# Local and global attention followed by an RWKV feed-forward: sigmoid as tanh, the softmax inverse and the squares moved to VectorE

## The chip, the core and the metric

The kernel runs on one core of a Trainium2 chip. A core has a matrix engine (PE, whose weight loads are listed apart as PEld), VectorE (DVE), ScalarE (ACT), GpSimd (POOL) and SyncE (SP, which issues the DMAs). Each engine works through its own queue strictly in order; semaphores tie the queues together. The metric is the device time of one execution in microseconds (us), lower is better.

## The reference

The attention has 8 batches, 8 heads, 512 local and 32 global positions, head dimension 64. A global query attends to everything; a local one to the 32 global keys and to local keys within 32 positions. Its output, joined over the heads, is the input of the feed-forward:

```
a = exp(s - max(s)) / (sum(exp(s - max(s))) + 1e-9)       # softmax, both kinds of query
x = attention output as (8, 576, 512)
xk = mu_k * x + (1 - mu_k) * x_prev                        # x_prev: one position earlier
xr = mu_r * x + (1 - mu_r) * x_prev
k = maximum(xk @ w_k, 0)                                   # 512 -> 1024
v = k * k @ w_v                                            # 1024 -> 512
out = 1 / (1 + exp(-(xr @ w_r))) * v
```

Everything is float32. The kernel keeps that accuracy by splitting each operand of a product into a high and a low part and adding three products.

## The kernel before

**Staging.** A unit is one batch and two heads; four units make a batch. While the heads of batch b are computed, the feed-forward of batch b-1 runs beside them; `together` interleaves the two generator streams in program order. From batch 2 on (`FROM`) the value product is done for two halves of 256 tokens at once by a Strassen scheme (class `Keys`), which needs sums and differences of the squared keys (`differences`, L624). At the end the 32 global tokens of all batches go through the feed-forward.

**What orders the work.** The kernel is written with a tile framework that schedules the whole program itself: it takes the instructions, simulates their progress on the engines with its own costs, and writes each engine's queue. So an edit in one line can move instructions everywhere. `tc.high_priority()` brings an instruction forward.

**The softmax of a unit** (`scores`). PE writes eight score blocks into four PSUM banks (L351). VectorE adds the mask, scales and takes the minimum of the negated scores (L320, eight times). ScalarE computes eight exponentials with their sums (L326). For each half `e` of the eight blocks `inverse` is called once: ScalarE adds 1e-9 to four sums (L283), VectorE takes the reciprocal (L284), and POOL multiplies the half by it (L335, a large and a small piece). PE then transposes the four blocks of each half (L372) into a bank, which ScalarE (half 0) or VectorE (half 1) copies out (L374), and two more blocks (L381) follow through the same banks. `scores_global` does the like for the global queries (L399 to L409).

**The feed-forward.** `mix` forms xk and xr on VectorE (L509, L513) and splits them (ScalarE L517, POOL L518). Products go into PSUM banks of the tag "m": two in the first stage, three from batch 2 on, seven at the very end. For the keys, ScalarE takes relu out of the bank. In batches 0 and 1 (`keys_and_gate`) POOL squares it in SBUF (L532) and ScalarE squares it again for the high part (L535). From batch 2 on (`squares`) ScalarE's relu (L551) goes to SBUF and POOL squares it there (L552). The bank is free when ScalarE has read it.

**The gate** (`gates`). For batch 0 ScalarE takes the sigmoid straight from each of the two banks (L564). For all later tokens VectorE copies each bank to SBUF (L568) and ScalarE takes one sigmoid over both (L570). ScalarE's functions come in sets, and only one set is loaded: a change between exponential and sigmoid is an instruction of its own, ACT_TABLE_LOAD, which the compiler places. `write` and `values` multiply gate and value (L582, L590) and store.

**Weights.** Each chunk of weights arrives as 64-bit words and is decoded by ScalarE (L190), VectorE (L191 to L197), ScalarE (L203) and POOL (L204); three buffers take turns, so the next load waits for POOL's last step.

Of the kernel before, what the change touches and what calls it, by code (L numbers as in the profile page):

```python
# [9 lines left out]
F32 = mybir.dt.float32  # L10
# [5 lines left out]
AF = mybir.ActivationFunctionType  # L16
# [3 lines left out]
P = 128  # L20
# [35 lines left out]
def local_global_attention_then_rwkv_ffn(  # L56
# [12 lines left out]
    nc = tc.nc  # L69
# [5 lines left out]
    scale = 1.0 / D ** 0.5  # L75

    const = ctx.enter_context(tc.tile_pool(name="const", bufs=1))
# [60 lines left out]

    mu_k_sb = const.tile([P, NC], F32, name="mu_k_sb")
    mu_r_sb = const.tile([P, NC], F32, name="mu_r_sb")  # L140
    eps = const.tile([P, 1], F32, name="eps")
    nc.vector.memset(eps, 1e-9)


    xg_all = const.tile([P, NC, GB, SG + 1], F32, name="xg_all")
# [76 lines left out]
    HC = NF // 2  # L222
# [57 lines left out]

    def inverse(ssum):

        nc.scalar.activation(ssum, ssum, AF.Identity, bias=eps)  # L283
        nc.vector.reciprocal(ssum, ssum)  # L284
        return ssum

# [10 lines left out]
    def scores(slots):  # L297

        r = Scores(slots)
        Pt = att2.tile([P, 8, WG], F32, tag="Pt", name="Pt")  # L300
        Pgl = att2.tile([P, 2, 4, SG], F32, tag="Pgl", name="Pgl")
        low_x = small.tile([P, 8], F32, tag="m", name="m")
        ssum = small.tile([P, 8], F32, tag="ssum", name="ssum")

        banks = [psum("s") for _ in range(4)]

        def place(e, t, h):
            return banks[2 * h + e][:, t * WG:(t + 1) * WG]
        run = Run(reads["s"] if slots[0][0].b > 1 else None)
        for t, (s, p) in enumerate(slots):  # L310
            for e in range(2):
                for a, i in enumerate(PAIRS[e][p]):
                    for h in range(2):
                        rows = slice(h * D, (h + 1) * D)
                        run.matmul(
                            place(e, t, h)[a * BL:(a + 1) * BL], s.q[rows, i * BL:(i + 1) * BL],
                            s.k[rows, START[i]:START[i] + WG], start=True, stop=True,
                        )
        for e, t, h, i in EACH:
            read = nc.vector.tensor_tensor_reduce(  # L320
                out=Pt[:, i], in0=place(e, t, h), in1=masks[:, e, slots[t][1]], op0=ALU.add, op1=ALU.min,
                scale=-scale, scalar=HUGE, accum_out=low_x[:, i:i + 1],
            )
        reads["s"] = [read]
        for e, t, h, i in EACH:
            nc.scalar.activation(  # L326
                Pt[:, i], Pt[:, i], AF.Exp, bias=low_x[:, i:i + 1], scale=-1.0, accum_out=ssum[:, i:i + 1],
            )
        for e in range(2):
            each = slice(4 * e, 4 * e + 4)  # L330
            rinv = inverse(ssum[:, each])
            window = Pt[:, each, SG * e:SG * e + W]
            for out, at in ((window, SG * e), (Pgl[:, e], 0 if e else W)):
                n = out.shape[2]
                nc.gpsimd.tensor_mul(out, Pt[:, each, at:at + n], rinv.unsqueeze(2).to_broadcast([P, 4, n]))  # L335
        r.Pt, r.Pgl = Pt, Pgl
        return r
# [150 lines left out]
    class Tokens:  # L488
# [29 lines left out]
                    nc.gpsimd.tensor_sub(lo[:, both], xf, hi[:, both].bitcast(F32))  # L518
            (_, self.xk_h, self.xk_l), (_, self.xr_h, self.xr_l) = got

        def keys_and_gate(self, whole_gate=True):

            self.kk_h, self.kk_l = [], []
            for f0 in range(0, NF, 2):
                kp = psum("m").rearrange("p (j n) -> p j n", j=2)
                for j in range(2):
                    products(kp[:, j], wk_h, wk_l, slice((f0 + j) * P, (f0 + j + 1) * P),
                             lambda c: self.xk_h[:, c], lambda c: self.xk_l[:, c], NC)
                rk = self.two(tmpp, "relu")
                nc.scalar.activation(rk, kp, AF.Relu)  # L530
                k2 = self.two(tmpp, "k2")
                nc.gpsimd.tensor_mul(k2, rk, rk)  # L532
                kh = self.two(mlp, "kkh", F32R, f"kkh{f0}")
# [6 lines left out]
            yield from self.gates(whole_gate)  # L540

        def squares(self, k2):

            for f0 in range(0, NF, 2):
                kp = psum("m").rearrange("p (j n) -> p j n", j=2)
                for j in range(2):
                    products(kp[:, j], wk_h, wk_l, slice((f0 + j) * P, (f0 + j + 1) * P),
                             lambda c: self.xk_h[:, c], lambda c: self.xk_l[:, c], NC)
                rk = self.two(tmpp, "relu")
                with tc.high_priority():  # L550
                    nc.scalar.activation(rk, kp, AF.Relu)  # L551
                nc.gpsimd.tensor_mul(k2[f0 // HC][f0 % HC // 2], rk, rk)  # L552
                yield

        def gates(self, whole_gate=True, pool=None):
            pool = pool or gatep
            self.gate = pool.tile([P, NC, TOK], F32, tag="gate", name="gate")
            for e0 in range(0, NC, 2):
                rp = psum("m").rearrange("p (j n) -> p j n", j=2)
                for j in range(2):  # L560
                    products(rp[:, j], wr_h, wr_l, slice((e0 + j) * P, (e0 + j + 1) * P),
                             lambda c: self.xr_h[:, c], lambda c: self.xr_l[:, c], NC)
                if not whole_gate:
                    nc.scalar.activation(self.gate[:, e0:e0 + 2], rp, AF.Sigmoid)  # L564
                    yield
                    continue
                with tc.high_priority(None if pool is not gatep else 0):
                    nc.vector.tensor_copy(self.gate[:, e0:e0 + 2], rp)  # L568
                if e0 + 2 == NC:
                    nc.scalar.activation(self.gate, self.gate, AF.Sigmoid)  # L570
                yield

        def values(self):
# [224 lines left out]
    def tokens_of(b):  # L798
        return [local_tokens(b, half, [xT_of(b, c) for c in range(NC)]) for half in range(2)]
# [21 lines left out]
    keys = [t.keys_and_gate(whole_gate=False) for t in first]  # L821
    decoding = weights(range(EARLY), wk_h, wk_l, "m")

    def by_halves(pair, p):
# [124 lines left out]
    t, = final.tokens  # L949
# [74 lines left out]
```

## Time and profile before

| | us |
|---|---|
| three timed runs | 713.49, 715.49, 715.31 (median 715.31) |
| profiled execution, its own time | 713.44 |
| its span in the profile | 711.6 |
| PE busy | 673.6 (95%) |
| VectorE, ScalarE, POOL busy | 404.2, 421.2, 412.1 |
| granted PE clock, mean over the span | 0.976 |

Busy time is the sum of an engine's instructions without overlap. A group of instructions is shown with its line, engine, operation, output and inputs, count, busy time and mean duration, and then with the idle time of that engine just before these instructions and what ended it. The stage tables give each engine's busy time in a stretch of the span, the granted clock of PE (1.00 is full) and the share of the DMA engines.

### The profile page before, as it was taken

To read this page: it belongs to the slowest core of one execution; us is meant where nothing else is said; L and a number is where in the kernel's file an instruction comes from. 1 tells how busy PE (TensorE), PEld (TensorE's weight loads), DVE (VectorE), ACT (ScalarE), POOL (GpSimd) and SP (SyncE) were. 2 spreads that over 40 slices of the span, in tenths; PEclk is the share of its full clock that TensorE was granted. 3 is DMA by queue.
4 is the path that set the end of the run, shared out by engine and by line. 5 is a ranking of instruction groups with operands and counts; after the bars stand their busy time and mean duration, and the time that the engine had idled before them with its cause. 6 is when DMAs were issued, how large, how long until landed. Compare 5 with 4: busy or idle time off the path is not lost.

```text
span 711.6 us, 18686 instructions
## 1 busy us (share of the span) xinstructions
PE 673.6 (95%) x7472; PEld 629.5 (88%) x7472; DVE 404.2 (57%) x1180; ACT 421.2 (59%) x1135; POOL 412.1 (58%) x415
## 2 busy tenths in 40 slices
PE   5779899998999999899999999999999999999997
PEld 3558788888999999889999999999989999999896
DVE  5757986535635473755665465726673557276341
ACT  5857786646656557755748384857466654442430
POOL 6556597785534356575557656575559434854820
PEclk9679999999999999999999999999999999999999
DMA  8631678554312541271918174544736090544665
GB/s 346 277 119 43 240 213 285 197 186 130 138 56 96 180 162 72 98 258 44 357 47 309 49 284 161 220 138 174 273 115 242 2 354 3 193 137 147 198 193 201
DMA packets 43543, 123.37 MB, mean 173 GB/s; under 512 B 4032, under 2 KB 20928, under 8 KB 43456
## 3 DMA queue, kind: packets, MB, share of 16 engines
q1 hardware_dynamic: 43456, 122.18, 48.7%
q8 instruction: 59, 0.97, 0.5%
q14 instruction: 28, 0.23, 0.1%
HBM read 104.86 MB, written 17.30 MB: 172 GB/s over the span
## 4 chain that ended last, share of the span: by engine, by line
PE 56%; ACT 13%; DVE 9%; POOL 8%; DMA 6%; issue 6%; SPq 0%; POOLq 0%; ACTq 0%; DVEq 0%
PE ps_m L643 13%; PE ps_m L486 9%; PE ps_m L485 9%; PE ps_m L484 9%; PE ps_s L351 8%; ACT Pt L326 4%; DVE xfull L513 3%; DMA w<-w_v 3%; PE ps_t L372 2%; POOL B L552 2%; DVE diff L509 2%; POOL Pt L335 1%; DMA w<-w_r 1%; PE ps_s L353 1%; DVE B L624 1%
## 5 line engine op out<-in xcount | busy, mean ns | idle before, releaser
L484 PE MATMUL ps_m<-xkh,wk_h 128*128 128x256 f32 x544 | 154.2, 285 | 6.7 <-ACT xkh L517 2.4
L485 PE MATMUL ps_m<-xkl,wk_h 128*128 128x256 f32 x544 | 152.0, 280 | 1.3 <-POOL xkl L518 1.3
L486 PE MATMUL ps_m<-xkh,wk_l 128*128 128x256 f32 x544 | 152.3, 280 | 0.0
L643 PE MATMUL ps_m<-bh,a 128*128 128x256 f32 x736 | 137.8, 283 | 1.5 <-DMA a<-scratch 0.8
L643 PEld LDWEIGHTS ps_m<-bh,a 128*128 128x128 f32 x736 | 115.6, 190 | 3.4 <-issue 1.6
L326 ACT ACTIVATE Pt<-Pt,m 128x160 f32<-128x160 f32 x256 | 106.5, 419 | 16.4 <-DVE m L320 13.9
L484 PEld LDWEIGHTS ps_m<-xkh,wk_h 128*128 128x128 f32 x544 | 102.7, 189 | 9.5 <-ACT xkh L517 2.9
L335 POOL TENSOR_TENSOR Pt<-Pt,ssum 128x512 f32<-128x512 f32 x64 | 70.5, 1102 | 69.3 <-DVE ssum L284 66.7
L485 PEld LDWEIGHTS ps_m<-xkl,wk_h 128*128 128x128 f32 x544 | 102.9, 189 | 1.8 <-POOL xkl L518 1.8
L643 PE MATMUL ps_m<-bl,a 128*128 128x256 f32 x368 | 103.6, 281 | 0.0
L486 PEld LDWEIGHTS ps_m<-xkh,wk_l 128*128 128x128 f32 x544 | 102.8, 189 | 0.0
L518 POOL TENSOR_TENSOR xkl<-xfull,xkh 128x512 fp32r<-128x512 f32 x34 | 45.3, 1333 | 60.7 <-ACT xkh L517 45.7
L552 POOL TENSOR_TENSOR B<-relu 128x512 f32<-128x512 f32 x52 | 56.6, 1095 | 40.2 <-ACT relu L551 40.1
L484 PE MATMUL ps_m<-xrh,wr_h 128*128 128x256 f32 x272 | 79.1, 291 | 0.0
L486 PE MATMUL ps_m<-xrh,wr_l 128*128 128x256 f32 x272 | 78.5, 290 | 0.1
L485 PE MATMUL ps_m<-xrl,wr_h 128*128 128x256 f32 x272 | 77.9, 287 | 0.0
L551 ACT ACTIVATE relu<-ps_m 128x512 f32<-128x512 f32 x52 | 31.0, 595 | 76.2 <-PE ps_m L486 76.2
L643 PEld LDWEIGHTS ps_m<-bl,a 128*128 128x128 f32 x368 | 69.8, 190 | 0.6 <-issue 0.6
L320 DVE CUSTOM_DVE_ANT_0 Pt<-ps_s,masks 128x160 f32<-128x160 f32 x256 | 65.6, 317 | 3.2 <-PE ps_s L351 3.0
L509 DVE TENSOR_TENSOR diff<-xT 128x256 f32<-128x256 f32 x64 | 38.7, 642 | 32.7 <-ACT xT L476 18.9
L203 ACT CAST bh<-B 128x512 fp32r<-128x512 f32 x76 | 45.5, 625 | 16.3 <-PE ps_m L643 13.8
L486 PEld LDWEIGHTS ps_m<-xrh,wr_l 128*128 128x128 f32 x272 | 52.5, 193 | 3.0 <-issue 2.8
(144 smaller groups left out, 1631.5 us busy)
## 6 DMA issues: line engine op xcount, KB each, us to landing
a<-scratch SPq DMA_DIRECT2D x92, 512.0 KB, 5.8
raw_qk<-qk SPq DMA_DIRECT2D x32, 768.0 KB, 5.5
raw_v<-v SPq DMA_DIRECT2D x32, 640.0 KB, 5.1
out_l<-gate SPq DMA_DIRECT2D x32, 256.0 KB, 4.7
w<-w_k SPq DMA_DIRECT2D x8, 512.0 KB, 9.9
w<-w_v SPq DMA_DIRECT2D x8, 512.0 KB, 5.5
w<-w_r SPq DMA_DIRECT2D x4, 512.0 KB, 4.6
scratch<-wv_h SPq DMA_DIRECT2D x8, 256.0 KB, 4.0
```

The source lines that it names most:

```text
L203: nc.scalar.copy(hi, val)
L320: read = nc.vector.tensor_tensor_reduce(out=Pt[:, i], in0=place(e, t, h), in1=masks[:, e, slots[t][1]], op0=ALU.add, op1=ALU.min, scale=-s ...
L326: nc.scalar.activation(Pt[:, i], Pt[:, i], AF.Exp, bias=low_x[:, i:i + 1], scale=-1.0, accum_out=ssum[:, i:i + 1],)
L335: nc.gpsimd.tensor_mul(out, Pt[:, each, at:at + n], rinv.unsqueeze(2).to_broadcast([P, 4, n]))
L351: self.last = nc.tensor.matmul(*a, **kw)
L484: nc.tensor.matmul(out, w_h[:, i, cols], x_h(i), start=(i == 0), stop=False)
L485: nc.tensor.matmul(out, w_h[:, i, cols], x_l(i), start=False, stop=False)
L486: nc.tensor.matmul(out, w_l[:, i, cols], x_h(i), start=False, stop=(i == n - 1))
L509: nc.vector.tensor_sub(self.shape(diff[:, j]), self.cur(c0 + j), self.prev(c0 + j))
L518: nc.gpsimd.tensor_sub(lo[:, both], xf, hi[:, both].bitcast(F32))
L552: nc.gpsimd.tensor_mul(k2[f0 // HC][f0 % HC // 2], rk, rk)
L643: nc.tensor.matmul(out[:, j], w, x[:, i % 2], start=fresh and (i, j, n) == (0, 0, 0), stop=(i, n) == (HC - 1, 2), skip_group_check=True,)
```

## The change

Three edits, and one consequence of the first:

- The gate is computed as 1/2 + tanh(x/2)/2. ScalarE takes the tanh with scale 0.5 straight from each PSUM bank, and then one Copy with scale 0.5 and bias 0.5 over the whole gate. This holds for all tokens; the special case of batch 0 and VectorE's copy out of the bank are gone.
- `inverse` adds 1e-9 on VectorE. In `scores` it is called once for all eight sums, after the eighth exponential, where it was called for each half.
- From batch 2 on the square of the keys is a product of the PSUM bank and relu, on VectorE with high priority, where it was a product of relu with itself on POOL. The bank is then free when VectorE has read it.

Names of the tiles and all other functions stay. Line numbers behind the edits fall by one to four.

```diff
-    eps = const.tile([P, 1], F32, name="eps")
-    nc.vector.memset(eps, 1e-9)
...
     def inverse(ssum):
-        nc.scalar.activation(ssum, ssum, AF.Identity, bias=eps)
+        nc.vector.tensor_scalar_add(ssum, ssum, 1e-9)
         nc.vector.reciprocal(ssum, ssum)
         return ssum
...
+        all_inv = inverse(ssum)
         for e in range(2):
             each = slice(4 * e, 4 * e + 4)
-            rinv = inverse(ssum[:, each])
+            rinv = all_inv[:, each]
...
                 rk = self.two(tmpp, "relu")
                 with tc.high_priority():
                     nc.scalar.activation(rk, kp, AF.Relu)
-                nc.gpsimd.tensor_mul(k2[f0 // HC][f0 % HC // 2], rk, rk)
+                with tc.high_priority():
+                    nc.vector.tensor_mul(k2[f0 // HC][f0 % HC // 2], kp, rk)
                 yield
...
-                if not whole_gate:
-                    nc.scalar.activation(self.gate[:, e0:e0 + 2], rp, AF.Sigmoid)
-                    yield
-                    continue
                 with tc.high_priority(None if pool is not gatep else 0):
-                    nc.vector.tensor_copy(self.gate[:, e0:e0 + 2], rp)
+                    nc.scalar.activation(self.gate[:, e0:e0 + 2], rp, AF.Tanh, scale=0.5)
                 if e0 + 2 == NC:
-                    nc.scalar.activation(self.gate, self.gate, AF.Sigmoid)
+                    nc.scalar.activation(self.gate, self.gate, AF.Copy, scale=0.5, bias=0.5)
                 yield
```

The order in which the engines take their instructions moves with it. The first place is ScalarE's queue at the first gate of batch 0. (`Pt`, `Pg` are softmax weights, `w` a chunk of weights, `ps_m` a PSUM bank.) Before:

```order
L190 ACTIVATE w_856<-w_856 128x512
L564 ACT_TABLE_LOAD
L564 ACTIVATE gate<-ps_m 128x512
L283 ACTIVATE ssum<-ssum,eps 128x4
L517 CAST xrh<-xfull 128x512
L564 ACTIVATE gate<-ps_m 128x512
L374 COPY PT<-ps_t 128x512
L517 CAST xkh<-xfull 128x512
L407 ACT_TABLE_LOAD
L407 ACTIVATE Pg,ssumg<-Pg,mg 128x576
```

With the change:

```order
L324 ACTIVATE Pt,ssum<-Pt,m 128x160 x4
L564 ACTIVATE gate<-ps_m 128x512
L516 CAST xkh<-xfull 128x512
L516 CAST xrh<-xfull 128x512
L564 ACTIVATE gate<-ps_m 128x512
L373 COPY PT<-ps_t 128x512
L406 ACTIVATE Pg,ssumg<-Pg,mg 128x576
L566 ACTIVATE gate<-gate 128x1024
```

Both table loads and the inverse are gone from this stretch, and one instruction, L566, has come in. In the whole program there were 30 table loads; now there is one, the first.

The second place is VectorE's queue at the differences of the squared keys of batch 2, the first batch of the Strassen scheme (`B_...` and `T_...` are blocks of squared keys and their differences, `PT` is the copy out of the transposes' bank). Before:

```order
L284 RECIPROCAL ssum<-ssum 128x4 x2
L624 TENSOR_TENSOR B_3407<-B_3842,B_3407 128x512
L624 TENSOR_TENSOR B_3407<-B_3843,B_3407 128x512
L624 TENSOR_TENSOR T_4051<-B_3844,B_3407 128x512
L624 TENSOR_TENSOR B_3842<-B_3844,B_3842 128x512
L374 COPY PT<-ps_t 128x512
```

With the change:

```order
L551 TENSOR_TENSOR B_3808<-ps_m,relu 128x512
L281 TENSOR_SCALAR ssum<-ssum 128x8
L620 TENSOR_TENSOR B_3377<-B_3808,B_3377 128x512
L282 RECIPROCAL ssum<-ssum 128x8
L551 TENSOR_TENSOR B_3809<-ps_m,relu 128x512
L620 TENSOR_TENSOR B_3377<-B_3809,B_3377 128x512
L551 TENSOR_TENSOR B_3810<-ps_m,relu 128x512
L620 TENSOR_TENSOR T_4015<-B_3810,B_3377 128x512
L620 TENSOR_TENSOR B_3808<-B_3810,B_3808 128x512
L620 TENSOR_TENSOR B_3378<-B_3378,T_4015 128x512
L373 COPY PT<-ps_t 128x512
```

The three squares now stand between the differences that need them; the two steps of the inverse stand among them too, and one more difference is ahead of the copy.

The third place is POOL's queue at the same squares. Before:

```order
L552 TENSOR_TENSOR B_3842<-relu 128x512
L335 TENSOR_TENSOR Pt<-Pt,ssum 128x4x128
L335 TENSOR_TENSOR Pgl<-Pt,ssum 128x128
L335 TENSOR_TENSOR Pt<-Pt,ssum 128x4x128
L335 TENSOR_TENSOR Pgl<-Pt,ssum 128x128
L552 TENSOR_TENSOR B_3843<-relu 128x512
L552 TENSOR_TENSOR B_3844<-relu 128x512
L552 TENSOR_TENSOR B_3845<-relu 128x512
L204 TENSOR_TENSOR bl<-T_4051,bh 128x512
```

With the change:

```order
L334 TENSOR_TENSOR Pt<-Pt,ssum 128x4x128
L334 TENSOR_TENSOR Pgl<-Pt,ssum 128x128
L334 TENSOR_TENSOR Pt<-Pt,ssum 128x4x128
L334 TENSOR_TENSOR Pgl<-Pt,ssum 128x128
L202 TENSOR_TENSOR bl<-T_4015,bh 128x512
```

The four squares have left the queue; the softmax multiplications and the split of T stand in the same order.

More of the change, by code (lines that the diff above doesn't have):

```diff
@@ L519, in mix, with keys_and_gate @@
             (_, self.xk_h, self.xk_l), (_, self.xr_h, self.xr_l) = got
-        def keys_and_gate(self, whole_gate=True):
+        def keys_and_gate(self):
             self.kk_h, self.kk_l = [], []
@@ L539, in keys_and_gate @@
                 yield
-            yield from self.gates(whole_gate)
+            yield from self.gates()
         def squares(self, k2):
@@ L551, in squares, with gates @@
                     nc.scalar.activation(rk, kp, AF.Relu)
-                nc.gpsimd.tensor_mul(k2[f0 // HC][f0 % HC // 2], rk, rk)
+                with tc.high_priority():
+                    nc.vector.tensor_mul(k2[f0 // HC][f0 % HC // 2], kp, rk)
                 yield
-        def gates(self, whole_gate=True, pool=None):
+        def gates(self, pool=None):
             pool = pool or gatep
@@ L820, in local_global_attention_then_rwkv_ffn @@
     first = tokens_of(0)
-    keys = [t.keys_and_gate(whole_gate=False) for t in first]
+    keys = [t.keys_and_gate() for t in first]
     decoding = weights(range(EARLY), wk_h, wk_l, "m")
```

## The prediction

> **What bounds the kernel now.** I read the page's busy times first, then the stages, then what PE waited for, then the time lines around three stalls.
>
> ```profile
> PE 673.6 (95%) x7472; PEld 629.5 (88%) x7472; DVE 404.2 (57%) x1180; ACT 421.2 (59%) x1135; POOL 412.1 (58%) x415
> ```
>
> PE is busy for 95% of the span and no other engine for more than 59%. The table by stage has length, then busy time of PE, its weight loads, DVE, ACT and POOL, then the granted clock, the DMA share and GB/s.
>
> ```profile
> 0.00:60.00 60.00, 42.70 (x413) 30.45 (x414) 39.84 (x147) 38.96 (x127) 34.27 (x55) 0.80 0.58 220
> 60.00:180.00 120.00, 110.97 (x1242) 100.16 (x1241) 77.65 (x235) 84.25 (x236) 86.48 (x87) 0.99 0.58 192
> 180.00:660.00 480.00, 474.85 (x5455) 454.83 (x5454) 272.28 (x780) 283.94 (x752) 271.84 (x258) 1.00 0.45 161
> 660.00:711.60 51.60, 45.03 (x371) 44.09 (x369) 14.45 (x21) 14.04 (x23) 19.53 (x16) 0.97 0.59 194
> 640.00:660.00 20.00, 20.00 (x176) 20.00 (x175) 13.76 (x20) 4.67 (x8) 10.67 (x9) 1.00 0.53 163
> ```
>
> PE is idle for 17.3, 9.0, 5.2 and 6.6 us in the four stages. In the last row it does nothing but large products, 176 in 20 us, 0.114 us each, without a gap. So from 180 to 660 us the products set the time, and the change removes none of them; it can win only the few stalls in there, those of the first 180 us, and one near 660. What PE waited for (total, times, longest):
>
> ```profile
> PE ps_t L422 <- ACT PTg L382: 5.7, 2, 3.3
> PE ps_t L381 <- DVE PT L374: 1.9, 1, 1.9
> PE ps_m L484 <- ACT gate L564: 1.6, 2, 1.4
> PE ps_m L484 <- ACT sum L668: 1.5, 1, 1.5
> PE ps_m L486 <- POOL wv_l L204: 1.1, 1, 1.1
> PE ps_m L484 <- DVE gate L568: 1.1, 1, 1.1
> PE ps_t L372 <- POOL Pt L335: 0.7, 1, 0.7
> PE ps_m L643 <- ACT sum L661: 0.6, 1, 0.6
> ```
>
> Rows two, three and six are waits for things that the change moves.
>
> **The change in busy time.** The groups that carry it:
>
> ```profile
> L570 ACT ACT_TABLE_LOAD x12 | 15.4, 1283 | 0.2
> L283 ACT ACTIVATE ssum<-ssum,eps 128x4 f32<-128x4 f32 x64 | 18.1, 291 | 0.1
> L570 ACT ACTIVATE gate<-gate 128x1024 f32<-128x1024 f32 x15 | 15.9, 1059 | 6.5 <-DVE gate L568 6.4
> L564 ACT ACTIVATE gate<-ps_m 128x512 f32<-128x512 f32 x4 | 2.4, 597 | 0.0
> L568 DVE COPY gate<-ps_m 128x512 f32<-128x512 f32 x30 | 20.4, 681 | 3.3 <-PE ps_m L486 3.3
> L284 DVE RECIPROCAL ssum<-ssum 128x4 f32<-128x4 f32 x64 | 10.7, 172 | 52.9 <-ACT ssum L283 52.7
> L582 DVE TENSOR_TENSOR gate<-ps_m,gate 128x512 f32<-128x512 f32 x8 | 5.5, 686 | 9.4 <-PE ps_m L486 9.4
> L552 POOL TENSOR_TENSOR B<-relu 128x512 f32<-128x512 f32 x52 | 56.6, 1095 | 40.2 <-ACT relu L551 40.1
> ```
>
> ACT loses 29 of 30 table loads (29 x 1.283 = 37.2 us), 80 inverses (64 here and 16 of the global queries, at 0.291: 23.3) and the sigmoids (15.9 + 2.4); it gains 34 tanh from PSUM, priced as the sigmoid from PSUM (34 x 0.597 = 20.3), and 17 Copies of the gate, priced as the sigmoid of that size (17 x 1.059 = 18.0). Net about -40 us. DVE gains 52 squares with one operand in PSUM, priced as the product of a bank and the gate (52 x 0.686 = 35.7), and 48 additions, no dearer than a reciprocal (48 x 0.172 = 8.3 at most, nothing at least); it loses 30 copies (20.4) and 32 reciprocals (5.5). Net about +18. POOL loses 56.6. None of this is on PE, so it counts only through the stalls.
>
> **The stall at 287 us.** The time lines of POOL, DVE and PE, and the stage right behind:
>
> ```profile
> 281.93 3.48 POOL L552 TENSOR_TENSOR B<-relu 128x512 f32<-128x512 f32 x3
> 283.00 1.51 DVE L624 TENSOR_TENSOR B<-B,B 128x512 f32<-128x512 f32 x1 [3.64 <-POOL B L552]
> 286.49 0.68 DVE L374 COPY PT<-ps_t 128x512 f32<-128x512 f32 x1
> 287.22 0.44 PE L381 MATMUL ps_t<-ident,Pgl 128*128 128x128 f32 x2 [1.93 <-DVE PT L374]
> 288.00:292.00 4.00, 4.00 (x24) 4.00 (x23) 4.00 (x15) 2.10 (x10) 0.00 (x0) 0.57 0.00 0
> ```
>
> POOL squares late, because softmax multiplications are ahead of the squares in its queue. DVE sits 3.64 us at a difference that needs a square, the next ones are slow while POOL works, and the copy that PE needs is behind them. The gap of 1.93 us also lowers the granted clock to 0.57 for the next 4 us: 4 x 0.43 = 1.7 us more. With the change the squares stand on DVE itself at 0.69 us, so neither the wait nor the slow difference has a cause. Gain 3.6 us; at least 0, if the copy stays late behind three squares. The Trainium skill (TensorE: Matmul & The Clock Gate, Part 1) lets the clock fall only after an idle window of about 3.4 us. By that rule this gap would cost 1.9 us and not 3.6; the trace shows the lower clock behind a shorter gap, and I go by the trace. By the rule, for all three stalls with a lower clock, the time would come out some 5 us above my sum.
>
> **The stall at 85 us.**
>
> ```profile
> 83.55 1.28 ACT L564 ACT_TABLE_LOAD   x1
> 84.85 0.60 ACT L564 ACTIVATE gate<-ps_m 128x512 f32<-128x512 f32 x1
> 80.00:100.00 20.00, 18.22 (x153) 15.59 (x152) 15.52 (x51) 19.79 (x58) 14.79 (x16) 0.91 0.70 225
> 112.62 1.28 ACT L564
> 114.53 1.28 ACT L326
> 125.14 1.28 ACT L564
> ```
>
> Only here is ACT full: 19.79 of 20 us. PE waits 1.6 us for the gate's bank behind a table load, and the clock of 0.91 costs another 1.8. Tanh needs no load here, so I take 3.4, at least 0. The last three rows are from the chain of waits: three more loads, 3.8 us, lie on it between 112 and 127 us, with the decoding of the weights behind them on ACT and POOL (the 1.1 us on wv_l). The rest of this stage's idle time, 9.0 - 1.6 = 7.4 us, partly hangs on DMA and on POOL's sums, which stay. I take 2.5 of it; bounds 0 and 7.4. The Trainium skill (ScalarE: Activation LUTs, What ACT_TABLE_LOAD costs) puts a drain of 1.38 us on top of the 1.283. The rows show none: the load begun at 83.55 ends at 84.83 and the sigmoid starts at 84.85. By the page the four loads named would give back 4 x 1.38 = 5.5 us more, and the time would come out that much below my sum.
>
> **The stall at 662 us.**
>
> ```profile
> 661.36 0.68 DVE L568 COPY gate<-ps_m 128x512 f32<-128x512 f32 x1
> 662.07 1.06 ACT L570 ACTIVATE gate<-gate 128x1024 f32<-128x1024 f32 x1 [3.49 <-DVE gate L568]
> 664.00:668.00 4.00, 4.00 (x24) 4.00 (x22) 0.33 (x1) 2.82 (x6) 3.80 (x4) 0.58 0.41 133
> ```
>
> The gate's copy is late in DVE's queue; PE waits 1.1 us for the bank and 0.6 for the sum that ACT copies behind the sigmoid, and 4 x 0.42 = 1.7 us go to the clock: 3.4 in all. With the change ACT, idle for 3.49 us there, reads the bank. I take 3.0; at least 0.
>
> **Smaller ones.** The wait of 1.5 us for sum L668: ACT copies it behind casts that wait for DVE's mixing, which runs beside POOL's squares no longer. I take 1.0, bounds 0 and 1.5. In the first 60 us the 5.7 us on PTg end a chain of exponentials and inverses on ACT; ten inverses fewer are some 2 to 3 us of its time. I take 1.5; bounds -2, if the later first half (next) tells here, and 5.7.
>
> **What it costs.** The first half of a softmax now waits for two more exponentials.
>
> ```profile
> L326 ACT ACTIVATE Pt<-Pt,m 128x160 f32<-128x160 f32 x256 | 106.5, 419 | 16.4 <-DVE m L320 13.9 <-PE ps_m L643 2.3
> DVE PT L374 <- PE ps_t L372: 31.6, 12, 6.0
> ```
>
> Two at 0.42 us, less the 0.29 of one inverse: POOL starts some 0.5 us later in each of 32 softmaxes, 16 us at the worst; but PE waited for POOL's product once in the whole run, 0.7 us. The cover is the products that PE has between score blocks and transposes; where that is gone, each costs its 0.5. I take 1.5 us. The banks of the keys now wait for DVE, 0.69 us behind relu; with three banks PE fills two others first, 24 products each, 5.5 us, so a bank is late only if DVE is behind by more than 4 us. Behind a square on DVE stand the inverse (POOL waits for it) and the copy PT (PE does). DVE itself waited for PE before that copy, 31.6 us in 12 long waits, 2.6 each, room for three squares. I take 2.0 us for such waits; bounds 0 and 25 (below).
>
> **The sum.** Gains 3.6 + 3.4 + 2.5 + 3.0 + 1.0 + 1.5 = 15.0, costs 1.5 + 2.0 = 3.5: 11.5 us less. The profiled execution took 713.44 us, so 701.9; the median of the timed runs, 715.31, lies 1.9 above it and would become 703.8. I predict **703 us**. A measurement of this kernel can tell about 0.3%, 2.1 us, from no change.
>
> **Rivals.**
> - *The stalls only move (to 709 to 715 us).* The whole program is ordered anew, and behind the stalls named stand mixing, weights and POOL's sums, which are as slow as before. For it: 5 of the 9 us of the second stage have no table load right ahead. Against it: ACT has 40 us less to do and the three largest stalls have causes that are gone. Only the stalls at 85 and 287 us stay away, 7.0, and the costs of 3.5 come twice: 713.
> - *All of it goes (693 to 697 us).* All listed bounds: 3.6 + 3.4 + 7.4 + 3.4 + 1.5 + 5.7 = 25, less 3.5 and a rest that DMA holds, some 3: 713.4 - 18.5, 695. For it: POOL and ACT have room everywhere. Against it: loads of weights and the first inputs stay.
> - *VectorE's queue takes over (slower, about 724 us).* A square at the head of DVE's queue waits for its relu; the copy PT behind it is late and PE stalls as at 287 us, 3.6 us with the clock, in seven of the ten key phases that run beside heads: 25 us, against the 15 gained. It decides as soon as the copy comes later than the products between the transposes cover, some 26 of 0.114 us or 3.0 us. Against it: the 2.6 us that DVE waits there, and DVE at 57%.
>
> **Chances.** Forecast (697 to 709) 0.62; stalls move 0.18; all of it goes 0.12; slower 0.08. The likeliest is 703; a range of 696 to 712 leaves out most of the slower case, the upper part of the second and a part of the third, about 2 in 10 together. Faster by over 0.3% are the first, the third and half of the second: 0.83. Within 0.3%: the rest of the second and a little of the slower one: 0.10. Slower: 0.07.
>
> **What would show it.** Right: one table load; no PE wait of 1 us on gate or PT near 85, 287 and 662 us, and the clock at 1.00 there; from 180 to 660 us PE busy for the whole stage, which is then 3 to 5 us shorter; differences at 0.7 us each. Wrong: PE waits on DVE's square or on PT in each batch (then the cost of DVE's queue was set too low); a second stage as long as before with new waits for weights (then ACT was not what held it); squares well over 0.69 us.

## The result, and the profile after

The changed kernel takes **702.75 us** (median of 4 runs, 702.47 to 706.29) against 714.87 (4 runs, 713.49 to 715.49): a ratio of 0.9844, 95% interval 0.981 to 0.9879, so 12.1 us less. The forecast was 703 with a range of 696 to 712. The profiled execution took 702.47 us with a span of 700.6; before it was 713.44 and 711.6, so the two traces lie 11.0 us apart.

Busy times on the page of the changed kernel:

```profile
PE 667.4 (95%) x7472; PEld 629.2 (90%) x7472; DVE 417.7 (60%) x1217; ACT 387.9 (55%) x1058; POOL 357.2 (51%) x363
```

ACT fell by 33.3 us, POOL by 54.9, and DVE rose by 13.5. PE has the same 7472 instructions but is busy for 6.2 us less: of the 11.0 us between the traces only 4.8 are idle time of PE; for the rest it was busy for longer before with the same products, in part because of a lower granted clock (last section). The groups that carry it (count, then busy time and mean ns, then the idle time ahead of them):

```profile
L551 DVE TENSOR_TENSOR B<-ps_m,relu 128x512 f32<-128x512 f32 x52 | 35.8, 689 | 74.6 <-ACT relu L549 74.5
L620 DVE TENSOR_TENSOR B<-B,B 128x512 f32<-128x512 f32 x24 | 19.9, 829 | 0.2
L564 ACT ACTIVATE gate<-ps_m 128x512 f32<-128x512 f32 x34 | 20.1, 592 | 11.3 <-PE ps_m L485 11.3
L566 ACT ACTIVATE gate<-gate 128x1024 f32<-128x1024 f32 x17 | 18.0, 1058 | 0.4
```

The same table by stage as before (length, busy time of PE, its weight loads, DVE, ACT, POOL, granted clock, DMA share, GB/s):

```profile
0.00:60.00 60.00, 42.17 (x428) 31.17 (x429) 41.86 (x151) 37.89 (x122) 34.10 (x55) 0.77 0.58 220
60.00:180.00 120.00, 109.87 (x1237) 100.48 (x1237) 81.00 (x237) 76.82 (x215) 87.54 (x91) 0.99 0.56 192
180.00:660.00 480.00, 479.43 (x5510) 462.20 (x5509) 284.12 (x816) 264.47 (x708) 227.58 (x212) 1.00 0.46 166
660.00:700.60 40.60, 35.90 (x304) 35.33 (x303) 10.70 (x16) 8.77 (x14) 7.97 (x6) 1.00 0.59 189
```

PE's idle time in the first two stages is as it was (17.8 and 10.1 us, before 17.3 and 9.0). From 180 to 660 us it went from 5.2 to 0.6 us, and at the end from 6.6 to 4.7. What PE waited for (the rows that bear on the forecast):

```profile
PE ps_t L421 <- ACT PTg L381: 3.8, 2, 2.6
PE ps_m L483 <- ACT relu L528: 3.2, 2, 2.5
PE ps_m L483 <- ACT xkh L516: 2.8, 2, 2.0
PE ps_s L346 <- DVE m L318: 2.3, 2, 2.0
PE ps_m L485 <- POOL wv_l L202: 1.4, 1, 1.4
PE ps_m L483 <- ACT gate L564: 0.6, 1, 0.6
```

All of these lie before 162 us. The copy PT at 287 us, the sum near 313 us and the gate's bank near 662 us are no longer waited for. Where the time went is told best by four products of PE that mean the same in both programs: the last product with w_v of the first units, the first of the large products, and the first and last product with w_r of the last phase. The kernel before:

```profile
242.28 0.28 PE L486 MATMUL ps_m<-kkh,wv_l 128*128 128x256 f32 x1
...
294.08 0.28 PE L643 MATMUL ps_m<-bh,a 128*128 128x256 f32 x1
...
649.77 0.28 PE L484 MATMUL ps_m<-xrh,wr_h 128*128 128x256 f32 x1
...
692.23 0.28 PE L486 MATMUL ps_m<-xrh,wr_l 128*128 128x256 f32 x1
```

The changed kernel:

```profile
240.79 0.28 PE L485 MATMUL ps_m<-kkh,wv_l 128*128 128x256 f32 x1
...
289.18 0.28 PE L639 MATMUL ps_m<-bh,a 128*128 128x256 f32 x1
...
642.00 0.28 PE L483 MATMUL ps_m<-xrh,wr_h 128*128 128x256 f32 x1
...
681.10 0.28 PE L485 MATMUL ps_m<-xrh,wr_l 128*128 128x256 f32 x1
```

| stretch | before | after | gain |
|---|---|---|---|
| start to last w_v product | 242.28 | 240.79 | 1.5 |
| to first large product (stall at 287) | 51.80 | 48.39 | 3.4 |
| to first w_r product of the last phase | 355.69 | 352.82 | 2.9 |
| to last w_r product (stall at 662) | 42.46 | 39.10 | 3.4 |
| to the end of the span | 19.4 | 19.5 | -0.1 |

Most of the gain is in the three stretches after 242 us. The first third, where the forecast put about half of its net gain, gave 1.5 us.

### The profile page after: what moved, and what is told of

Its sections match the earlier page's. It is cut to its first block, busy times and chain, and to the rows that moved or that the text cites. A ratio compares the mean times of both kernels' runs of the same rounds, so it can differ in the third digit from the quotient of the medians.

```text
span 700.6 us, 18622 instructions
## 1 busy us (share of the span) xinstructions
PE 667.4 (95%) x7472; PEld 629.2 (90%) x7472; DVE 417.7 (60%) x1217; ACT 387.9 (55%) x1058; POOL 357.2 (51%) x363
## 4 chain that ended last, share of the span: by engine, by line
PE 75%; DMA 7%; POOL 6%; ACT 5%; DVE 4%; issue 2%; SPq 0%; POOLq 0%; ACTq 0%; DVEq 0%
PE ps_m L639 16%; PE ps_m L483 14%; PE ps_m L484 13%; PE ps_m L485 13%; PE ps_s L350 9%; DMA a<-scratch 3%; PE ps_t L371 3%; ACT Pt L324 2%; PE ps_s L352 2%; DMA w<-w_r 2%; DMA w<-w_v 1%; POOL Pt L334 1%; PE ps_t L421 1%; PE ps_t L350 1%; PE ps_t L380 1%
## 5 line engine op out<-in xcount | busy, mean ns | idle before, releaser
L484 PE MATMUL ps_m<-xkl,wk_h 128*128 128x256 f32 x544 | 154.0, 283 | 0.4 <-POOL xkl L517 0.4
L639 PE MATMUL ps_m<-bh,a 128*128 128x256 f32 x736 | 139.5, 283 | 1.3 <-DMA a<-scratch 1.2
L334 POOL TENSOR_TENSOR Pt<-Pt,ssum 128x512 f32<-128x512 f32 x64 | 68.6, 1072 | 79.7 <-ACT xrh L516 23.2
L517 POOL TENSOR_TENSOR xkl<-xfull,xkh 128x512 fp32r<-128x512 f32 x34 | 46.9, 1379 | 99.3 <-ACT xkh L516 94.3
L551 DVE TENSOR_TENSOR B<-ps_m,relu 128x512 f32<-128x512 f32 x52 | 35.8, 689 | 74.6 <-ACT relu L549 74.5
L639 PEld LDWEIGHTS ps_m<-bl,a 128*128 128x128 f32 x368 | 69.2, 188 | 0.0
L586 POOL TENSOR_TENSOR gate<-sum,gate 128x512 f32<-128x512 f32 x18 | 26.7, 1481 | 59.3 <-DVE sum L685 38.4
L201 ACT CAST bh<-B 128x512 fp32r<-128x512 f32 x76 | 46.0, 620 | 18.2 <-PE ps_m L639 12.1
L483 PEld LDWEIGHTS ps_m<-xrh,wr_h 128*128 128x128 f32 x272 | 52.2, 192 | 3.2 <-ACT relu L528 2.6
```

What stands on the lines that cost most here:

```text
L201: nc.scalar.copy(hi, val)
L483: nc.tensor.matmul(out, w_h[:, i, cols], x_h(i), start=(i == 0), stop=False)
L484: nc.tensor.matmul(out, w_h[:, i, cols], x_l(i), start=False, stop=False)
L551: nc.vector.tensor_mul(k2[f0 // HC][f0 % HC // 2], kp, rk)
L639: nc.tensor.matmul(out[:, j], w, x[:, i % 2], start=fresh and (i, j, n) == (0, 0, 0), stop=(i, n) == (HC - 1, 2), skip_group_check=True,)
```

## Experiments: one part alone

The theory behind the forecast gives each stall its own edit: the squares end the stall at 287 us and the wait for the sum, the gate edit those at 85 and 662 us, the inverse almost nothing. Rival one: ScalarE's relief, by the table loads, is all of it. Rival two: any re-ordering moves stalls about. Three kernels make one edit each on the kernel before. The gate alone:

```
-                if not whole_gate:
-                    nc.scalar.activation(self.gate[:, e0:e0 + 2], rp, AF.Sigmoid)
...
-                    nc.vector.tensor_copy(self.gate[:, e0:e0 + 2], rp)
+                    nc.scalar.activation(self.gate[:, e0:e0 + 2], rp, AF.Tanh, scale=0.5)
...
-                    nc.scalar.activation(self.gate, self.gate, AF.Sigmoid)
+                    nc.scalar.activation(self.gate, self.gate, AF.Copy, scale=0.5, bias=0.5)
```

> The gate's edit alone, on the kernel before. Theory (each stall has its own edit): the waits on gate and sum near 662 us go with their lower clock (3.4 us), the wait at 85 us shrinks, the stall on PT near 287 us stays (1.9 us and the clock); 706 to 710 us where the kernel before takes 714.5. Rival one (ScalarE's relief by 37 us of table loads is the whole gain): 702 to 704. Rival two (any new order moves the stalls, the edit itself does little): 712 to 716, with stalls at other places.

The inverse alone:

```
-        nc.scalar.activation(ssum, ssum, AF.Identity, bias=eps)
+        nc.vector.tensor_scalar_add(ssum, ssum, 1e-9)
...
+        all_inv = inverse(ssum)
...
-            rinv = inverse(ssum[:, each])
+            rinv = all_inv[:, each]
```

> The inverse's edit alone (on VectorE, once per unit). Theory: no stall hangs on it; 713 to 716 us, the stalls at 85, 287 and 662 us stay. Rival one: ScalarE is relieved of 23 us, less than of table loads; 709 to 712. Rival two: anything from 710 to 718 with other stalls. If the later first half of the softmax costs its 0.5 us each time: up to 730.

The later squares alone:

```
-                nc.gpsimd.tensor_mul(k2[f0 // HC][f0 % HC // 2], rk, rk)
+                with tc.high_priority():
+                    nc.vector.tensor_mul(k2[f0 // HC][f0 % HC // 2], kp, rk)
```

> The squares' edit alone (from batch 2 on from PSUM on VectorE). Theory: the stall on PT near 287 us goes with its clock (3.5 us), and VectorE's mixing runs freer, so the 1.5 us on sum near 313 us shrink too; the stalls at 85 and near 662 us stay; 709 to 712 us. Rival one: no change, 713 to 716, since ScalarE has as much to do. Rival two: 710 to 718. VectorE's queue taking over: above 720.

Against 715.51 us of the kernel before (median of 13 runs on the same chip):

| kernel | median, range | ratio, 95% interval |
|---|---|---|
| gate alone | 705.44, 704.80 to 706.13 | 0.9861, 0.9838 to 0.9884 |
| inverse alone | 715.11, 711.82 to 720.69 | 0.9999, 0.9973 to 1.0026 |
| squares alone | 710.51, 708.42 to 711.74 | 0.9925, 0.9900 to 0.9951 |

The gate earns 10 us, somewhat more than its theory had (706 to 710 us), the squares 5, the inverse nothing. Rival two falls for the gate, which lies far below its 712 to 716; for the squares and the inverse its wide ranges hold the measured times too, and only the waits below decide. Rival one falls, since the squares earn 5 us with 29 table loads still there. The squares edit changes engine, operand and priority at once; which of the three earns the 5 us was not tried.

But the theory of the stalls holds only in part. PE's waits in the profiled executions, from the lists of what PE waited for and its time lines (a dash: under 0.3 us; one profile of each kernel):

| wait of PE, us | before | inverse | squares | gate | whole |
|---|---|---|---|---|---|
| gate's bank near 85 | 1.4 | 2.0 | 1.6 | - | 0.6 |
| copy PT near 287 | 1.9 | 1.9 | - | - | - |
| sum near 313 | 1.5 | 1.4 | - | 1.4 | - |
| gate's bank near 662 | 1.1 | 0.9 | 0.5 | - | - |
| relu between 92 and 102 | - | - | 1.7 | 2.0 | 3.2 |

The wait for the gate's bank near 662 us shrinks without the gate edit too: with the squares alone it is 0.5 us and not 1.1. The sum behaves as forecast: it is still waited for with the gate edit alone, whose list of PE's waits has

```profile
PE ps_m L484 <- ACT sum L664: 1.4, 1, 1.4
```

and gone wherever the squares are on VectorE. The stall at 287 us does not: either edit ends it. In the kernel with the gate edit alone, POOL still squares. DVE's and PE's time lines there:

```profile
279.62 1.51 DVE L620 TENSOR_TENSOR B<-B,B 128x512 f32<-128x512 f32 x1 [3.65 <-POOL B L552]
280.74 0.60 PE L372 MATMUL ps_t<-ident,Pt 128*128 128x128 f32 x4
282.26 0.68 DVE L374 COPY PT<-ps_t 128x512 f32<-128x512 f32 x1
```

DVE waits 3.65 us for a square, and the difference takes 1.51 us, both as before. But these stand mostly ahead of the transposes: the copy starts 1.5 us after PE has begun them, and PE still has products. Before, PE began the transposes at about the same point of the batch:

```profile
281.70 0.60 PE L372 MATMUL ps_t<-ident,Pt 128*128 128x128 f32 x4
```

and the copy followed at 286.49, 4.8 us later, because the wait fell between the two. So the late square was a real link, but the stall needed it to fall in just that place.

## Experiments: the whole without one part

Each of these is the changed kernel with one edit undone. Without the inverse edit:

> The gate's and the squares' edit, with the inverse as before (ScalarE adds, once per half). Theory: the time of the whole change, 701 to 705 us, since no stall hangs on the inverse. Rival one: 704 to 707 (23 us of ScalarE come back). Rival two: 700 to 710 with other stalls in the first 180 us.

Without the squares (on POOL, from relu, as before):

> The gate's and the inverse's edit, with the squares on POOL as before. Theory: a stall on PT or on a difference behind POOL's square near 287 us, as before; 705 to 709 us, some 4 above the whole change. Rival one (ScalarE's relief is all): 702 to 704, as the whole change. Rival two: 702 to 712 with stalls at other places.

Without the gate edit (sigmoid, VectorE's copies and table loads as before):

> The squares' and the inverse's edit, with the sigmoid and its table loads as before. Theory: the waits on gate and sum near 662 us are back (3.4 us with the clock), the one at 85 us too; 708 to 712 us. Rival one: no gain left but that of 23 us of inverses, 711 to 715. Rival two: 706 to 716.

The first was timed against the 715.51 us above, the other two on another chip against 715.66 (16 runs).

| kernel | median, range | ratio, 95% interval |
|---|---|---|
| whole without inverse | 701.85, 699.85 to 703.22 | 0.9805, 0.9780 to 0.9830 |
| whole without squares | 706.38, 705.43 to 709.70 | 0.9881, 0.9847 to 0.9914 |
| whole without gate | 710.49, 707.14 to 711.99 | 0.9928, 0.9902 to 0.9953 |

All three medians lie where the theory put them, but two of its mechanisms do not show. Without the squares edit the copy PT near 287 us was to be late again: PE waits nowhere 0.3 us there. Without the gate edit the stall at 662 us was to come back with 3.4 us: PE waits 0.3 us for the gate's bank and 0.7 for the sum, at full clock. Only the wait near 85 us came back as said (2.0 us). Gate and squares add up: 10.1 + 5.0 = 15.1 us alone, 13.7 together (715.51 - 701.85). That the sum is a little short agrees with the stall at 287 us, which both end. The inverse again adds nothing to the squares (710.49 against 710.51) and rather takes from the gate (706.38 against 705.44).

## Experiments: what in the gate edit earns it

The gate edit does two things: no table loads, and ACT instead of DVE as the reader of the banks. Two kernels keep one of them. The first has ACT read each bank with the sigmoid, so the loads stay:

```
-                    nc.scalar.activation(self.gate[:, e0:e0 + 2], rp, AF.Tanh, scale=0.5)
-                if e0 + 2 == NC:
-                    nc.scalar.activation(self.gate, self.gate, AF.Copy, scale=0.5, bias=0.5)
+                    nc.scalar.activation(self.gate[:, e0:e0 + 2], rp, AF.Sigmoid)
```

> The whole change, but the gate is a sigmoid taken straight from each bank (no tanh, no Copy, no copy by VectorE): the table loads are back, one or two at each gate, the banks' reader is ScalarE as in the change. It separates the table loads from the change of the banks' reader. Theory: near 662 us no wait on gate, since no exponential is left there and one load is covered; in the first 180 us the wait on gate near 85 us is back; 703 to 708 us. Rival one: all of the gate's gain is lost, 709 to 714.

Measured: 716.60 us (10 runs, 715.17 to 720.60), ratio 1.0017, interval 0.9997 to 1.0036. The theory missed by 8.6 us, the rival by 2.6. The two places came as the theory said: PE waits 2.0 us for the gate near 85 us and not for it near 662. What it had left out lies between them. The groups of table loads:

```profile
L564 ACT ACT_TABLE_LOAD x24 | 30.8, 1283 | 0.4
L324 ACT ACT_TABLE_LOAD x12 | 15.4, 1283 | 1.2 <-DVE m L318 1.0
L406 ACT ACT_TABLE_LOAD x11 | 14.1, 1283 | 0.2
L188 ACT ACT_TABLE_LOAD x1 | 1.3, 1283 | 0.7 <-PEq L1006 0.7
```

48 loads instead of 30. A sigmoid for each bank lands between exponentials, twice for a gate where the collected sigmoid landed there once. ACT and PE around one of them:

```profile
370.39 1.28 ACT L564 ACT_TABLE_LOAD   x1
371.68 0.60 ACT L564 ACTIVATE gate<-ps_m 128x512 f32<-128x512 f32 x1
372.30 1.28 ACT L324 ACT_TABLE_LOAD   x1
373.60 0.43 ACT L324 ACTIVATE Pt<-Pt,m 128x160 f32<-128x160 f32 x1
...
374.43 0.24 ACT L422 COPY PG<-ps_t 128x128 f32<-128x128 f32 x1
374.73 0.27 PE L352 MATMUL ps_s<-PT,raw_v 128*64 128x64 f32 x1 [1.34 <-ACT PG L422]
```

Two loads and one sigmoid, 3.2 us, stand ahead of the copy PG, and PE waits 1.34 us for it. Such waits for PG or for the maxima behind it recur about every 39 us, at 335, 375, 414, 454, 493, 532 and 572 us. From 320 to 660 us PE was busy for 331.7 of 340 us, against 339.1 in the whole without the gate edit, which has the copies and the collected sigmoid. So a table load in the middle of a head, which my forecast took as free in the steady state, is not free once two come in a row.

The second has DVE copy the banks as before, and then one tanh and one Copy on the whole tile, so there is one table load in the run:

```
-                    nc.scalar.activation(self.gate[:, e0:e0 + 2], rp, AF.Tanh, scale=0.5)
+                    nc.vector.tensor_copy(self.gate[:, e0:e0 + 2], rp)
                 if e0 + 2 == NC:
+                    nc.scalar.activation(self.gate, self.gate, AF.Tanh, scale=0.5)
                     nc.scalar.activation(self.gate, self.gate, AF.Copy, scale=0.5, bias=0.5)
```

> The whole change, but VectorE copies each bank of the gate to SBUF as before, and ScalarE takes one tanh and one Copy over the whole: no table loads, the banks' reader is VectorE. It is the other half of that separation. Theory: the wait on gate near 662 us is back, since the copy stands late in VectorE's queue; 704 to 708 us. Rival one (only the table loads count): 702 to 704.

Measured: 710.66 us (5 runs, 706.81 to 711.58), ratio 0.9920, interval 0.9891 to 0.9948; by medians that is what the whole without the gate edit takes, 710.49, and above both forecasts (704 to 708, 702 to 704). The profiled execution was the shortest of the five, 706.81, so its trace can explain only part of it: PE is busy for 477.1 us of those from 180 to 660, against 479.4 in the changed kernel, and waits 0.30 us for the gate's copy and 0.66 for the sum near 657, the remains of the stall at 662. What follows is that neither half of the edit earns the 7 to 8 us alone: with the loads gone and DVE still the reader, little or nothing is gained; with ACT the reader and 48 loads, 6 us are lost. But that kernel has more loads than the 30 before, so it doesn't show what ACT as the reader is worth with the loads as they were; a kernel in which ACT only copies each bank and takes one sigmoid for both was not tried.

## Experiments: the inverse once more, and the first 130 us

The whole and the whole without the inverse had not been timed side by side. Both were run again on one chip, beside two kernels that also take the squares of the first two batches from PSUM on VectorE:

```
-                nc.gpsimd.tensor_mul(k2, rk, rk)
+                nc.vector.tensor_mul(k2, kp, rk)
```

These test the new wait for relu. In the changed kernel's time lines:

```profile
98.88 2.38 DVE L534 TENSOR_TENSOR kkl<-k,kkh 128x512 fp32r<-128x512 f32 x1
101.29 0.60 ACT L528 ACTIVATE relu<-ps_m 128x512 f32<-128x512 f32 x1 [2.22 <-DVE kkl L534]
101.94 0.39 PE L483 MATMUL ps_m<-xrh,wr_h 128*128 128x256 f32 x1 [2.51 <-ACT relu L528]
```

The tiles of relu, squares and mixing share buffers in turn. A relu waits until a residue (kkl) has been written, which took 2.38 us beside POOL's work (0.68 to 0.69 where POOL rests), and PE waits for the relu.

> The whole change, timed on the same chip as the three versions beside it. Theory (the gate and the squares of the later keys earn everything, the inverse earns nothing): 702 to 704 us. Rival (the earlier 702.75 us was low by the choice of the few runs): 704 to 707.

> Gate and squares, the inverse as in the kernel before (one for each half, half of it on ScalarE), on the same chip as the whole change. Theory one (the merged inverse makes the first half of each softmax later and costs what ScalarE's shorter queue gives): within 1 us of the whole change. Theory two (the merged inverse costs by itself, about 1 us, in the first 60 us, where PE waits 2.04 us for the score maxima at 16.70 with it and not without it): 1 to 2 us faster than the whole change. Theory three (the inverse helps, as forecast for the first 60 us): 1 to 2 us slower.

> The whole change, and the squares of the first two batches' keys on VectorE from PSUM as well (32 products of 128x512 move from POOL, 1.04 us each, to VectorE, about 0.69 us each). Theory (the new waits of 0.67 and 2.51 us for relu at 92 and 102 us come because POOL's square and a slow difference of 2.38 us beside POOL hold relu's buffer; without POOL's square they go): 1 to 3 us faster than the whole change, no wait for relu over 1 us before 110 us. Rival (VectorE's queue before 180 us is the tight one; the squares delay score maxima and copies): the same as the whole change or up to 4 us slower, with more PE waits for VectorE's maxima.

> Gate edit and squares of all keys on VectorE from PSUM, the inverse as in the kernel before. If the early squares remove the relu waits and the inverse earns nothing: 699 to 701 us, the fastest of the four. If VectorE's queue before 180 us is the tight one: 702 to 706, slower than gate and later squares alone.

| kernel, against 714.14 us (9 runs) | median, range | ratio, 95% interval |
|---|---|---|
| whole | 703.53, 701.79 to 705.31 | 0.9848, 0.9825 to 0.9871 |
| whole without inverse | **700.16**, 698.78 to 701.64 | 0.9804, 0.9783 to 0.9826 |
| whole, early squares too | 702.45, 701.21 to 704.00 | 0.9834, 0.9811 to 0.9857 |
| without inverse, early squares too | 703.81, 702.30 to 704.85 | 0.9850, 0.9828 to 0.9872 |

Without the inverse edit the kernel is 3.4 us faster by medians, and the ranges don't touch (in the earlier runs it was 0.9 us, with ranges that overlap). So the edit costs something like 1 to 3 us inside the whole, though by itself it changes nothing. Theory two had the sign, not the size (1 to 2 us), and its place is wrong: the wait of 2.0 us for the maxima at 16.7 us is real, yet the first product with w_k starts earlier with the edit, at 48.8 us in the changed kernel and 51.1 without it. The lead is mostly gone by the first product with w_r (69.2 and 70.1 us). Of the pair timed side by side, the whole is level with the other at the score products at 199 us, 0.7 us behind at 413, 1.3 at 453 and 0.6 at 489. Then the whole has this wait of PE for a tile reloaded from memory,

```profile
495.81 0.35 PE L639 MATMUL ps_m<-bh,a 128*128 128x256 f32 x1 [1.40 <-DMA a<-scratch]
```

and at the next score products it is 2.7 us behind (511.3 against 508.5). In the earlier pair that wait is 0.5 us, and at these score products the whole is 1.2 us ahead, so this wait is not the edit's steady price. One part of it is steady in both pairs, and it is no wait: from the score products near 199 us to those near 337, and again from those near 550 us to the first product with w_r of the last phase, PE is busy throughout at full clock with the same products. The first stretch takes 137.98 and 137.99 us with the inverse edit and 137.41 and 137.43 without it, the second 92.35 both times with it and 91.80 both times without. So PE itself takes about 0.55 us longer in each; why is not shown. Where the rest goes is not settled, and whether the merging of the halves or the change of engine does it was not tried.

The early squares do remove the wait for relu, and little or nothing is won: the whole is 1.1 us faster by medians, with ranges that overlap, and the kernel without the inverse edit 3.7 us slower. In the whole with early squares, ACT and PE:

```profile
122.44 0.62 ACT L516 CAST xkh<-xfull 128x512 fp32r<-128x512 f32 x1 [3.33 <-DVE xfull L512]
122.97 0.59 ACT L564 ACTIVATE gate<-ps_m 128x512 f32<-128x512 f32 x1
123.61 0.58 PE L483 MATMUL ps_m<-kkh,wv_h 128*128 128x256 f32 x1 [3.09 <-ACT gate L564]
```

VectorE's mixing is now late, ACT stands behind it, and the gate's bank behind ACT: the wait of 2.51 us for relu has gone, and one of 3.09 stands 22 us later. That wait of 2.51 us is not firm either: in the second trace of the whole PE waits 0.6 and 0.9 us for relu, and 2.2 instead of 1.4 for the weights (wv_l). The fastest kernel of all is thus the gate edit with the later squares.

## Why the prediction was right, step by step

The time came out where it was forecast, but through two errors of about 4 us that cancel. That the number is so close is luck: the stalls after 180 us came out about as sized, the terms for the first 180 us and for VectorE's queue did not.

- **Busy time.** DVE +13.5 (forecast +18; its own terms came to +21, since the additions took 9.9 us, above the bound of 8.3, and the reciprocals lost 4.3 and not 5.5, while mixing and the splitting of the squared blocks, which I had left as they were, took some 12 us less), POOL -54.9 (-56.6), ACT -33.3 (-40). Tanh at 592 ns and Copy at 1058 ns are as priced, and so is the square at 689. The miss on ACT fits the inverses: I took 0.291 us for each of 80, but they overlap what follows. In the kernel with gate and later squares, one of them and the next instruction on ACT:

```profile
94.67 0.29 ACT L283 ACTIVATE ssum<-ssum,eps 128x4 f32<-128x4 f32 x1
94.86 0.64 ACT L203 CAST wv_h<-w 128x512 fp32r<-128x512 f32 x1
```

  The next starts 0.19 us later; 80 x 0.10 = 8 us.
- **Stall at 287 us, 3.6.** Measured 3.4 by the table of stretches. The step "the squares stand on DVE itself, so the wait has no cause" is right as far as it goes; that the squares alone would do it is not: the gate edit ends it too, with the late square still there.
- **Stalls at 85 us and on the loads up to 127 us, 3.4 + 2.5, with 1.5 for the first 60 us less 1.5 for the later first half: 5.9 forecast, 1.5 measured by 242 us. This step failed.** The cause I named is gone in the main: PE waits 0.6 us instead of 1.4 for the gate near 85 us. The sentence on the rest of the stage's idle time was where the risk stood, and the first rival described it: the wait for relu is new (3.2 us), the one for wv_l grew from 1.1 to 1.4, and the one for the cast xkh near 160 us, 1.8 before and 2.0 now, brings down the clock, 1.7 us more, where the wait near 85 us did so before. In the first 60 us the granted clock is 0.77 against 0.80, but 0.83 in the second trace of the same kernel, so that part is not the edits' doing. So the stage is no shorter though ACT does less in it: 76.8 us of work instead of 84.3.
- **Stall at 662 us, 3.0.** Measured 3.4, and the gate edit alone ends the waits. But half of the 3.4 is the clock, which this edit is not needed for: with the inverse alone the waits there are 0.9 and 0.6 us and with the squares alone 0.5 and 0.7, and in neither trace does the clock fall.
- **The sum, 1.0.** The 1.5 us went whole, with the squares. The stretch around it gained 2.9, of which before's waits of 0.31, 1.50 and 0.42 us between 301 and 340 us, less a new one of 0.49 at 493 us, explain 1.7; the rest lies in a PE that is busy throughout.
- **Waits behind squares in DVE's queue, 2.0. This term was over-sized:** after 162 us PE waited nowhere 0.2 us for DVE. A square never takes more than 0.69 us (below), and DVE's waits for relu (74.5 us in all) held up nobody that PE waits for. The slower rival was the same worry, and nothing of it came.
- **The later first half, 1.5.** PE waits nowhere for POOL's product, as the cover promised; yet the edit costs 1 to 3 us, in part in a PE that doesn't wait at all and for the rest in a place that the runs don't settle, where the forecast had balanced it with a gain of 1.5 in the first 60 us.
- **What would show it.** One table load, no wait of 1 us at 287 and 662 us, the third stage 4.6 us less idle: as said. "Differences at 0.7 us each": wrong, the mean of the largest group rose from 766 to 829 ns, and that of all 48 went from 769 to 778.

## What to carry to other kernels

Before moving work off an engine, ask of each stall whether the next resource in line (shared buffers, weights, another queue) is late by nearly as much: where several are, as in the first 180 us here, the first relief earns little; where one late link stands alone in front of an engine that is otherwise full, as at 313 and 662 us, it earns all of it. Time each part of a bundled edit both alone and left out, since a part that is neutral alone, as the inverse here, can cost in company. A function that shares the loaded table, put straight on the engine that has room, was worth more than either step alone.

## What the runs showed of the hardware

**An operand in PSUM keeps VectorE out of POOL's way.** DVE and POOL in the changed kernel:

```profile
275.70 0.69 DVE L551 TENSOR_TENSOR B<-ps_m,relu 128x512 f32<-128x512 f32 x1 [0.48 <-ACT relu L549]
276.42 0.92 DVE L620 TENSOR_TENSOR B<-B,B 128x512 f32<-128x512 f32 x1
285.64 1.73 DVE L620 TENSOR_TENSOR T<-B,B 128x512 f32<-128x512 f32 x1
275.39 1.04 POOL L334 TENSOR_TENSOR Pt<-Pt,ssum 128x512 f32<-128x512 f32 x1 [4.92 <-DVE ssum L282]
276.75 1.49 POOL L334 TENSOR_TENSOR Pt<-Pt,ssum 128x512 f32<-128x512 f32 x1
285.53 1.29 POOL L517 TENSOR_TENSOR xkl<-xfull,xkh 128x512 fp32r<-128x512 f32 x1 [2.79 <-ACT xkh L516]
```

All 52 squares take 0.68 or 0.69 us, 12 of them beside POOL for more than half of their time. The 48 differences, whose operands both lie in SBUF, take 0.68 or 0.69 when POOL rests (32) and 0.68 to 1.73, 0.97 on average, when it works (16). Half of these 16 take 0.68 or 0.69 there too, so POOL's work doesn't always slow them. The closest comparison is beside the same softmax multiplication (L334): four differences take 0.92 to 1.33, ten squares 0.69. And the differences did not get faster because, though POOL squares no longer, 16 still run beside its other work, where 19 ran beside POOL before (0.90 on average). The Trainium skill (GPSIMD Engine Reference, 1. Specifications) says the two engines share their SBUF interfaces, with contention for DVE instructions that have two SBUF inputs; the trace agrees.

**The clock does not go by the length of one gap.** The changed kernel around the wait of 2.51 us that ends at 101.94 us and around that of 1.99 us that ends at 160.25 (the clock is the last but two of each row):

```profile
97.20:100.61 3.41, 2.23 (x22) 1.85 (x20) 3.41 (x4) 1.78 (x4) 3.41 (x3) 1.00 0.19 63
100.61:104.02 3.41, 2.08 (x15) 1.80 (x17) 2.12 (x5) 2.70 (x6) 2.09 (x3) 1.00 0.98 268
104.02:107.43 3.41, 3.41 (x51) 2.75 (x49) 2.81 (x7) 2.24 (x5) 1.59 (x2) 1.00 0.94 257
158.64:162.05 3.41, 1.30 (x9) 1.09 (x10) 3.41 (x18) 2.36 (x7) 1.77 (x2) 1.00 0.83 287
162.05:165.46 3.41, 3.41 (x18) 3.41 (x18) 0.45 (x4) 3.41 (x16) 0.74 (x1) 0.50 0.03 10
```

The longer gap cost no clock, the shorter one half speed for 3.41 us, 1.7 us. In every trace the clock changes only at the marks of a fixed grid of 3.413 us, and the rows are cells of this trace's grid. The longer gap fell across a mark: PE idles 1.18 us in one cell and 1.33 in the next. The shorter one, with a gap of 0.50 us behind it, leaves PE idle for 2.11 us in one cell, and the next cell runs at half clock. Over the 14 traces, after 60 us and from cells at full clock: with 1.77 us or more of idle time in a cell the next was at half clock each time (21 cells), with 1.55 or less never (2559 cells), and in between 5 times out of 9. So a stall's price can double by where it falls on the grid, which no edit sets, and which lies elsewhere in each execution. The Trainium skill (TensorE: Matmul & The Clock Gate, Part 1) asks for an idle window of about 3.4 us, free-running; the length of the slow stretch agrees with that window, the need for it to be idle throughout does not agree with either drop seen here (1.93 us before, 1.99 now).

**A table load costs its 1.283 us and no more.** In the rows of the sigmoid on each bank, the load begun at 370.39 ends at 371.67 and the sigmoid starts at 371.68, the one at 372.30 ends at 373.58 and the exponential starts at 373.60. The drain of 1.38 us that the Trainium skill (ScalarE: Activation LUTs, What ACT_TABLE_LOAD costs) adds does not show.
